# Layer norm 2 on ScalarE: variance as centred squares, two GpSimd operations a pair, and a newly written order

## The chip, the cores and the metric

The kernel runs on one core of a Trainium2 chip. Its engines work side by side: TensorE (PE; its weight loads are listed as PEld), VectorE (DVE), ScalarE (ACT), GpSimd (POOL) and SyncE (SP), which here issues every transfer. The metric is the device time of one execution in microseconds, the median of several runs.

## The reference, cut to what matters

One input `x` (2048 tokens, 640 channels, bf16) goes through two branches, and a gate mixes them.

```python
g = sigmoid((x * gate_w).sum(-1, keepdims=True))
# branch A: a gated long convolution over the tokens
kv = (four-tap shift convolution of k with shift_k) * v
y  = irfft(rfft(kv padded to 2S) * rfft(ssm_k padded to 2S))[:S] + kv * ssm_D
a  = x * y
# branch B: a token-shift MLP
h  = gelu(layernorm(x) @ w1)
x1 = x + concat(four channel groups of h, shifted by 1, -1, 2, -2 tokens) @ w2
b  = x1 + gelu(layernorm(x1) @ w3) @ w4          # w3: 640x1536, w4: 1536x640
out = g * a + (1 - g) * b
```

`layernorm` subtracts the mean over the channels and divides by the root of the variance plus 1e-5. The second one, of `x1`, is "layer norm 2" here.

## The kernel before

Tokens lie as 128 partitions by 16 slabs; a slab `s` is 128 tokens by 640 channels. The work is cut into small named nodes, and the names carry the slab or chunk.

Branch B. `st0.s` are the statistics of layer norm 1, `rs0.s` the root for a pair of slabs, `xn0.s` the normalised slab. It is transposed into XNT, on TensorE (`tr`, evacuated by `te`) or by a transposing transfer (`xt0.c.i`). `W1.c.n` multiplies chunk `c` (four slabs) by w1, `g1` is the GELU, `mx` the shift of the mixed rest, `gt` and `z` the gate. `W2.s` multiplies by w2, and `add s` (L674) adds to QX and sums the row into SSM. Then `st1.s`, `rs1.s`, `xn1.s`, `xt1.c.i` are layer norm 2 with its transposes; its chunks begin with slabs 2, 6, 10 and 14. `W3.c.f` and `g2.c.f` follow, `W4.s.j` with the addition `w4e.s.j` (L784). `xo s` scales x1 by 1 - g.

Branch A computes the long convolution as a two-step discrete Fourier transform in matrix form. `trh`, `trhe` transpose the filter; `h1.c.u` is its first step, `he` the evacuation, `hw c` the write to DRAM. `km`, `ka`, `kv` are the shift convolution of k times v on VectorE (L828 to L840); `x1.c.u`, `xe`, `xw c` its first step. `rh` and `rx` read both back in another layout, `h2`, `x2` are the second step, evacuated by `h2e`, `x2e`. `sw` swaps two halves of the filter's spectrum by transfer. `pq` (L912) multiplies the spectra, `pv` starts the inverse, `ve` evacuates, `vw` writes, `rv` reads, `iv` ends the inverse, `ye`, `y`, `ya` gate and add it, `st s` stores.

What sets the order: no scheduler runs when the kernel is built. A string, ORDER, lists all nodes; a word is a name, an engine letter (P, A, V, G, S) and the places in the buffers that it uses. Each engine takes its nodes in the order of that string, one after the other, so a node that waits holds up all that stand behind it on its engine. SyncE's nodes are the issues of transfers, and what it issues runs in one queue. PSUM has eight places; an evacuation frees one or two of them for the next matmuls. The numbers in braces in `pl.add` ("plan times", ns) are what a planner outside this file used when it wrote ORDER; in the kernel they do nothing.

Layer norm 2 before: `st1` is one ScalarE instruction, a square scaled by D to the power of -1/2 with the row sum into SSQ. `rs1` is five GpSimd operations on 128x2: mean from SSM, its square, the difference from SSQ, plus epsilon, power of -1/2. `xn1` (L534, VectorE) subtracts the mean and multiplies by the root.

Of the kernel before, what the change touches and what calls it, by code (L numbers as in the profile page):

```python
# [9 lines left out]
ACT = mybir.ActivationFunctionType  # L10
ALU = mybir.AluOpType
# [74 lines left out]
h0/S bpi/V idn/G warm/P/0 iw/G cw/V is/G dz/G cs/V ang1/V and1/V sin1.1/A abs1/A sin1.0/A ang0/V and0/V sin0.1/A abs0/A  # L86
sin0.0/A q1/S st0.3/V st0.2/V h2/S h4/S q0/S st0.0/A m3i0/G trh0/P/2 trhe0/V/2 misc/G st0.1/V rs0.2/G xn0.3/V/0 xn0.2/V/1
trh2/P/4 trhe2/A/4 trh4/P/6 rs0.0/G h1/S q3/S st0.6/V st0.7/A rs0.6/G trh1/P/0 tr0.0.2/P/2/0/1/0 trhe1/A/0 trhe4/V/6 xn0.1/V/2
xn0.0/V/0 h3/S trh3/P/4 te0.0.2/V/2/0 tr0.0.0/P/6/0/0/2 te0.0.0/A/6/0 trhe3/V/4 h1.2.2/P/2/0 he.2.2/A/2/0 iz/G m3i1/G w1/S
h1.3.0/P/0/1 h1.2.0/P/4/0 he.2.0/A/4/0 W1.0.1/P/6/0 q2/S st0.5/V he.3.0/A/0/1 st0.4/V xn0.6/V/1 xn0.7/V/0 q4/S st0.9/V st0.8/V  # L90
q7/S h1.1.0/P/2/2 h1.2.1/P/4/0 he.1.0/A/2/2 W1.0.0/P/7/0 he.2.1/A/4/0 tr0.1.2/P/0/1/1/0 te0.1.2/V/0/1 rs0.4/G xn0.4/V/2
xn0.5/V/0 q5/S tri/S w2b2/S q6/S W1.0.2/P/2/0 W1.0.3/P/3/0 tr0.1.0/P/4/1/2/0 te0.1.0/V/4/1 w1m/G gw/S gt.0/P/0/0 rs0.8/G
xn0.9/V/1 st0.14/V g1.0.1/A/6 st0.12/V xn0.8/V/0 st0.15/A st0.11/A st0.10/V W1.0.4/P/1/0 z0/V/0 w2a/S st0.13/V g1.0.2/A/2
rs0.14/G W1.1.0/P/6/1 g1.1.0/A/6 g1.0.4/A/1 W1.1.4/P/4/1 g1.1.4/A/4 mx1.1/V mx0.1/V g1.0.0/A/7 g1.0.3/A/3 W1.1.3/P/2/1
g1.1.3/A/2 mx0.2/G rs0.10/G cjb/S drow/S hw2/S/0 W1.1.1/P/6/1 g1.1.1/A/6 w2b3/S kb1/S/0 xt0.2.1/S/0/1 w2b1/S mx1.3/V m3i3/G
xn0.11/V/2 w2b0/S xt0.2.0/S/0/0 h1.0.1/P/4/0 he.0.1/A/4/0 h1.1.2/P/0/2 he.1.2/A/0/2 k1.0/S/1 xt0.2.3/S/0/2 h1.3.2/P/2/1
he.3.2/V/2/1 xn0.10/V/1 mx0.0/G xt0.2.2/S/0/1 W1.1.2/P/7/1 g1.1.2/A/7 gt.1/P/6/1 h1.1.1/P/2/2 h1.0.2/P/4/0 he.0.2/A/4/0 z1/V/6
he.1.1/A/2/2 hw1/S/2 h1.3.1/P/0/1 xn0.14/V/0 xt0.3.2/S/1/0 W2.4/P/6 add4/V/6 W2.2/P/4 add2/V/4 W2.3/P/2 ka1/S/0 he.3.1/A/0/1
hw3/S/1 xn0.15/V/2 xt0.3.3/S/1/2 kb0/S/0 cj2/A cj0/A ic0/A W1.2.3/P/0/0 m3b/V g1.2.3/A/0 W1.2.1/P/1/0 st1.4/A g1.2.1/A/1 m3i2/G
m3i4/G cj3/G kz/V/0 rs0.12/G mx1.2/G mx1.0/G add3/V/2 xn0.12/V/1 xt0.3.0/S/1/1 xn0.13/V/0 xt0.3.1/S/1/0 gt.2/P/0/0 ka2/S/0  # L100
z2/V/0 ka0/S/0 cj1/A h1.4.2/P/6/2 he.4.2/A/6/2 h1.4.1/P/4/2 he.4.1/A/4/2 h1.0.0/P/2/0 he.0.0/A/2/0 hw0/S/0 W2.5/P/0 add5/V/0
ic1/V st1.5/A v0.1/S m3c/G m3d/V W1.2.4/P/6/0 g1.2.4/A/6 mx2.3/V h1.6.0/P/4/1 h1.6.1/P/0/1 he.6.1/V/0/1 he.6.0/A/4/1
h1.6.2/P/2/1 he.6.2/A/2/1 hw6/S/1 v0.0/S W1.2.2/P/7/0 g1.2.2/A/7 st1.2/A W1.2.0/P/6/0 st1.3/A gt.3/P/2/1 W1.3.4/P/3/1
g1.3.4/A/3 W1.3.0/P/7/1 g1.3.0/A/7 g1.2.0/A/6 W1.3.2/P/3/1 g1.3.2/A/3 z3/V/2 gate0/V gate1/A rs1.4/G xn1.5/V/2 xt1.0.3/S/0/2
W1.3.3/P/2/1 g1.3.3/A/2 w3/S h1.5.2/P/4/0 he.5.2/A/4/0 h1.5.1/P/0/0 he.5.1/A/0/0 h1.5.0/P/6/0 he.5.0/A/6/0 km0.0.3/V/0/0
km0.0.2/V/0/0 km0.0.1/V/0/1 xn1.4/V/1 ka0.0.2/V/0/0 gate2/V km0.0.0/V/0/0 ka0.0.1/V/1/0 ka0.0.0/V/0/0 rs1.2/G mx2.2/G
W1.3.1/P/3/1 g1.3.1/A/3 mx2.0/G xn1.2/V/0 kv0/V/0 xt1.0.2/S/0/1 W2.6/P/4 add6/V/4 xn1.3/V/2 xt1.0.1/S/0/2 h1.7.0/P/0/1
h1.4.0/P/6/2 mx2.1/G he.4.0/A/6/2 W2.7/P/2 add7/V/2 st1.7/A xt1.0.0/S/0/0 W2.8/P/6 W2.9/P/4 km0.1.3/V/0/0 km0.1.2/V/0/1
add8/V/6 he.7.0/A/0/1 st1.6/A mx3.1/G mx3.3/G W2.12/P/2 m3s/A mx3.2/G add9/V/4 mx3.0/G W2.11/P/0 h1.7.2/P/6/1 he.7.2/A/6/1
st1.8/A st1.9/A xo4/A add12/V/2 km0.1.1/V/0/0 ka0.1.2/V/1/0 ka0.1.1/V/0/0 rs1.6/G xn1.7/V/1 add11/V/0 km0.1.0/V/0/1  # L110
ka0.1.0/V/1/0 st1.12/A kv2/V/0 xn1.6/V/2 k1.1/S/1 km1.0.3/V/1/0 km1.0.2/V/1/0 ka1.0.2/V/0/0 km1.0.1/V/1/1 ka1.0.1/V/1/0
km1.0.0/V/1/0 ka1.0.0/V/0/0 v1.1/S v1.0/S kv4/V/0 h1.7.1/P/4/1 he.7.1/A/4/1 rs1.8/G xn1.9/V/0 mx0.3/G km1.1.3/V/1/0
km1.1.2/V/1/1 km1.1.1/V/1/0 ka1.1.2/V/1/0 w4/S xt1.1.0/S/1/2 W2.13/P/2 W3.0.11/P/6/0/0 g2.0.11/A/6/0 W3.0.3/P/7/0/1
W3.0.9/P/0/0/0 g2.0.3/A/7/1 g2.0.9/A/0/0 W3.0.6/P/1/0/2 W3.0.2/P/4/0/1 g2.0.2/A/4/1 xo3/A W3.0.1/P/5/0/1 xo6/A W3.0.0/P/0/0/1
g2.0.1/A/5/1 add13/V/2 xo7/A W3.0.4/P/4/0/2 g2.0.4/A/4/2 W3.0.5/P/5/0/2 g2.0.5/A/5/2 W3.0.7/P/4/0/2 g2.0.6/A/1/2 ka1.1.1/V/0/0
km1.1.0/V/1/1 g2.0.0/A/0/1 g2.0.7/A/4/2 W3.0.10/P/5/0/0 ka1.1.0/V/1/0 st1.11/A g2.0.10/A/5/0 W3.0.8/P/0/0/0 g2.0.8/A/0/0
kv6/V/0 xn1.8/V/2 st1.13/A rs1.12/G W2.10/P/6 add10/V/6 st1.10/A rs1.10/G k2.1/S/0 k2.0/S/0 km2.0.3/V/0/0 km2.0.2/V/0/0
xt1.1.1/S/1/1 v2.0/S v2.1/S xo9/A xo2/A ka2.0.2/V/0/0 xt1.1.3/S/1/0 W4.2.0/P/0/1/2/0 W4.3.1/P/1/1/2/0 km2.0.1/V/0/1
km2.0.0/V/0/0 W4.3.0/P/2/1/2/0 w4e3.1/V/1 w4e3.0/V/2 W4.2.1/P/3/1/2/0 W4.4.0/P/4/1/2/0 xt1.1.2/S/1/2 w4e2.1/V/3 ka2.0.1/V/1/0
ka2.0.0/V/0/0 xn1.13/V/1 w4e2.0/V/0 kv8/V/0 v3.0/S hw5/S/0 k3.1/S/1 W4.4.1/P/1/1/2/0 W4.5.1/P/5/1/2/0 xo5/A w4e5.1/V/5  # L120
W3.1.3/P/0/1/3 g2.1.3/A/0/3 W4.5.0/P/5/1/2/0 km2.1.3/V/0/0 km2.1.2/V/0/1 w4e4.1/V/1 w4e5.0/V/5 ka2.1.2/V/1/0 W3.1.1/P/0/1/3
hw4/S/2 W3.1.10/P/1/1/0 g2.1.10/A/1/0 xn1.12/V/0 g2.1.1/A/0/3 xt1.2.3/S/0/1 w4e4.0/V/4 W3.1.4/P/5/1/1 g2.1.4/A/5/1 k3.0/S/1
hw7/S/1 x1.0.2/P/6/0 x1.0.1/P/2/0 xe.0.1/A/2/0 x1.0.0/P/0/0 xe.0.0/A/0/0 xe.0.2/A/6/0 xw0/S/0 v3.1/S xn1.10/V/2 km2.1.1/V/0/0
xt1.2.0/S/0/2 km2.1.0/V/0/1 ka2.1.1/V/0/0 ka2.1.0/V/1/0 kv10/V/0 W3.1.5/P/4/1/1 g2.1.5/A/4/1 W3.1.0/P/5/1/3 g2.1.0/A/5/3
x1.1.0/P/2/2 xe.1.0/A/2/2 x1.1.2/P/0/2 W3.1.7/P/6/1/1 g2.1.7/A/6/1 xe.1.2/A/0/2 W3.1.8/P/7/1/0 g2.1.8/A/7/0 x1.1.1/P/4/2
xe.1.1/A/4/2 xw1/S/2 xn1.11/V/1 km3.0.3/V/1/0 xt1.2.1/S/0/1 xt1.2.2/S/0/0 km3.0.2/V/1/0 km3.0.1/V/1/1 ka3.0.2/V/0/0
x1.3.1/P/2/1 x1.3.0/P/0/1 xe.3.0/A/0/1 xe.3.1/V/2/1 ka3.0.1/V/1/0 km3.0.0/V/1/0 ka3.0.0/V/0/0 kv12/V/0 W3.1.9/P/6/1/0
g2.1.9/A/6/0 W3.1.2/P/7/1/3 g2.1.2/A/7/3 km3.1.3/V/1/0 km3.1.2/V/1/1 ka3.1.2/V/1/0 x1.4.0/P/4/0 xe.4.0/A/4/0 km3.1.1/V/1/0
km3.1.0/V/1/1 ka3.1.1/V/0/0 ka3.1.0/V/1/0 kv14/V/0 x1.4.1/P/2/0 xe.4.1/A/2/0 x1.4.2/P/0/0 xe.4.2/A/0/0 xw4/S/0 W3.1.6/P/6/1/1
g2.1.6/A/6/1 W3.1.11/P/7/1/0 x1.3.2/P/4/1 xe.3.2/A/4/1 xw3/S/1 x1.6.0/P/2/2 W2.0/P/0 xe.6.0/A/2/2 x1.6.1/P/4/2 x1.6.2/P/2/2  # L130
xe.6.2/A/2/2 xe.6.1/A/4/2 xw6/S/2 g2.1.11/A/7/0 xo10/A W3.2.0/P/6/0/2 g2.2.0/A/6/2 W2.1/P/2 add1/V/2 st1.1/A W3.2.1/P/7/0/2
xo8/V g2.2.1/A/7/2 rh1/S/0 add0/V/0 st1.0/A W2.15/P/4 x1.5.0/P/2/0 xe.5.0/A/2/0 x1.2.0/P/0/1 xe.2.0/A/0/1 add15/V/4 st1.15/A
W2.14/P/6 add14/V/6 st1.14/A W3.2.2/P/2/0/2 g2.2.2/A/2/2 rh0/S/1 x1.5.1/P/4/0 xe.5.1/V/4/0 x1.5.2/P/0/0 xe.5.2/V/0/0 xw5/S/0
# [43 lines left out]
def kernel(  # L177
# [16 lines left out]
    nc = tc.nc  # L194
# [808 lines left out]
```

## Time and profile before

| | |
|---|---|
| median of 5 runs | 231.18 us (228.54 to 232.07) |
| the profiled execution | 231.4 us |
| its span, first to last instruction | 229.6 us |
| granted TensorE clock | 0.994 |
| busy: PE, DVE, ACT, POOL | 212.9, 177.5, 170.3, 53.7 us |
| bytes moved | 65.39 MB, 285 GB/s on average |
| `rs1` and `rs0`: power of -1/2 (L527) | 16 of 824 ns on average |
| `rs1`: mean (L523) | 8 of 497 ns |
| `st1`: square (L507), its read of the sum | 16 of 738 ns, 16 of 193 ns |
| `xo`: copy with a pointer scale (L688) | 12 of 829 ns |
| gate activation, 128x16 (L640) | 1 of 208 ns |
| PSUM evacuation 128x1024, ScalarE, VectorE | 1.03 us (KV), 1.06 us on average (SX) |

Busy times say how full an engine is, not who holds up whom. TensorE is busy 93% of the span; the profile models the ends of its matmuls. A wait is told as "who <- what ended it". Start times below are microseconds from the span's start.

### The profile page before, as it was taken

What the parts mean: (1) busy time and instruction counts of PE and PEld (TensorE: products, weight loads), DVE (VectorE), ACT (ScalarE), POOL (GpSimd) and SP (SyncE); (2) the same over time, 40 slices, a digit from 0 to 9 for tenths busy, and PEclk for the clock granted to TensorE, in tenths of its full rate; (3) what the DMA queues carried; (4) which work ended last, traced back from release to release, by engine and by line L of the source; (5) the groups of instructions that cost most, each with busy time, mean ns of one, the idle gap of its engine ahead of it and who ended that gap; (6) DMA issues with size and microseconds to landing.
All of it is one profiled execution on the core that took longest, in us unless ns stands there. A gap on an engine that the chain in (4) does not pass through costs nothing.

```text
span 229.6 us, 4842 instructions
## 1 busy us (share of the span) xinstructions
PE 212.9 (93%) x1849; PEld 120.0 (52%) x1849; DVE 177.5 (77%) x311; ACT 170.3 (74%) x251; POOL 53.7 (23%) x129
## 2 busy tenths in 40 slices
PE   7999996999899998999999997997989999999990
PEld 7974553554654475644555554332435554466660
DVE  6799875579999999999996792778945887018991
ACT  5899995898399925169889941898997998517750
POOL 5276391659754057000004000000000000000000
PEclk9999999999999999999999999999999999999997
DMA  7999999989989999987999999999998949689995
GB/s 236 379 385 167 342 209 201 292 245 317 280 189 293 276 213 183 288 222 197 270 295 375 381 241 383 202 355 361 273 377 259 387 168 316 233 307 402 344 359 192
DMA packets 51095, 65.39 MB, mean 285 GB/s; under 512 B 20608, under 2 KB 37761, under 8 KB 50688
## 3 DMA queue, kind: packets, MB, share of 16 engines
q1 hardware_dynamic: 51072, 65.09, 97.8%
q8 instruction: 14, 0.23, 0.4%
q14 instruction: 9, 0.07, 0.1%
HBM read 37.03 MB, written 18.35 MB: 241 GB/s over the span
## 4 chain that ended last, share of the span: by engine, by line
PE 58%; DVE 19%; DMA 12%; issue 4%; SPq 3%; ACT 1%; DVEq 0%; POOL 0%; POOLq 0%
PE PS L778 15%; PE PS L765 14%; DMA R<-R 7%; PE PS L667 6%; PE PS L861 6%; DMA XNT<-XN 5%; PE PS L578 4%; PE PS L701 4%; DVE RK L833 4%; PE PS L726 4%; DVE RK L837 4%; SPq L541 3%; PE PS L946 2%; PE PS L472 2%; DVE XN L534 1%
## 5 line engine op out<-in xcount | busy, mean ns | idle before, releaser
L330 ACT CAST SX<-PS 128x1024 bf16<-128x1024 f32 (+1 forms) x58 | 51.3, 933 | 9.4 <-PE PS L861 7.8
L778 PE MATMUL PS<-W,RG 128*128 128x320 bf16 x384 | 56.0, 299 | 1.4 <-DVE QX L784 1.0
L765 PE MATMUL PS<-XNT,W 128*128 128x512 bf16 x240 | 56.0, 380 | 0.3 <-DMA XNT<-XN 0.2
L778 PEld LDWEIGHTS <-RG 128*128 128x128 bf16 x384 | 36.4, 98 | 21.2 <-issue 7.0
L769 ACT ACTIVATE RG<-PS 128x512 bf16<-128x512 f32 x48 | 28.2, 609 | 13.7 <-PE PS L765 13.4
L765 PEld LDWEIGHTS <-W 128*128 128x128 bf16 x240 | 22.0, 98 | 29.6 <-issue 5.4
L784 DVE SCALAR_TENSOR_TENSOR QX<-PS,ZG,QX 128x320 bf16<-128x320 f32 x32 | 17.0, 547 | 20.2 <-PE PS L778 17.7
L912 DVE TENSOR_TENSOR SX<-SX,R 128x2048 bf16<-128x2048 bf16 x20 | 23.8, 1221 | 7.0 <-DMA R<-R 5.9
L578 PE MATMUL PS<-XNT,R 128*128 128x512 bf16 x100 | 23.2, 379 | 2.3 <-DMA XNT<-XN 2.3
L667 PE MATMUL PS<-R 128*128 128x320 bf16 x160 | 23.7, 299 | 0.9 <-DVE QX L674 0.8
L837 DVE TENSOR_TENSOR RK<-RK 128x1280 bf16<-128x1280 bf16 x24 | 20.4, 851 | 0.4
L667 PEld LDWEIGHTS <-R 128*128 128x128 bf16 x160 | 15.3, 98 | 9.3 <-issue 3.1
L833 DVE TENSOR_TENSOR RK<-RK,CJ 128x1280 bf16<-128x1280 bf16 x24 | 19.1, 818 | 0.0
L507 ACT ACTIVATE RG<-QX 128x640 bf16<-128x640 bf16 x16 | 11.8, 738 | 9.2 <-DVE QX L674 9.1
L330 ACT CAST KV<-PS 128x1024 bf16<-128x1024 f32 x17 | 17.2, 1029 | 1.7 <-PE PS L861 1.6
L534 DVE TENSOR_SCALAR XN<-QX,MV,RS 128x640 bf16<-128x640 bf16 x32 | 14.3, 461 | 3.0 <-DMA XNT<-XN 2.6
L674 DVE SCALAR_TENSOR_TENSOR QX<-PS,QX 128x640 bf16<-128x640 f32 x16 | 12.9, 814 | 4.7 <-PE PS L667 4.5
L861 PEld LDWEIGHTS <-M 64*64 64x64 bf16 x320 | 7.9, 105 | 15.8 <-issue 8.5
L861 PE MATMUL PS<-RK,M 64*64 64x512 bf16 x160 | 13.9, 386 | 2.5 <-DMA RK<-GXD 2.5
L578 PEld LDWEIGHTS <-R 128*128 128x128 bf16 x100 | 9.1, 97 | 13.4 <-issue 3.6
L585 ACT ACTIVATE R<-PS 128x512 bf16<-128x512 f32 x20 | 11.2, 611 | 3.9 <-PE PS L578 3.9
L523 POOL TENSOR_SCALAR MV<-ST 128x2 f32<-128x2 f32 x8 | 4.0, 497 | 43.2 <-DVE QX L674 43.0
(116 smaller groups left out, 281.8 us busy)
## 6 DMA issues: line engine op xcount, KB each, us to landing
GHD<-SX SPq DMA_DIRECT2D x8, 640.0 KB, 6.2
GXD<-SX SPq DMA_DIRECT2D x8, 640.0 KB, 4.5
RK<-GHD SPq DMA_DIRECT2D x4, 1280.0 KB, 8.8
RK<-GXD SPq DMA_DIRECT2D x4, 1280.0 KB, 8.0
R<-R SPq DMA_DIRECT2D x8, 640.0 KB, 7.8
VD<-KV SPq DMA_DIRECT2D x4, 1280.0 KB, 7.0
W<-in_B_w_dram SPq DMA_DIRECT2D x2, 1920.0 KB, 11.1
RK<-in_A_k_dram SPq DMA_DIRECT2D x6, 560.0 KB, 7.6
```

Of the source, the lines that this page charges most:

```text
L330: nc.scalar.copy(out=o, in_=i)
L534: xn = pl.add("xn%d.%d" % (i, s), {V: 360}, lambda e: nc.vector.tensor_scalar(out=XN[:, b.idx, :], in0=QX[:, s, :], scalar1=MV[:, i, s, 0: ...
L578: nc.tensor.matmul(ps(pb), lhsT=lhsT, rhs=XNT[:, xb.idx, k, :], start=(k == 0), stop=(k == DT - 1))
L667: nc.tensor.matmul(ps(pb)[:, j, 0:DH], lhsT=gst_ap(k, s), rhs=W2[:, k, j * DH:(j + 1) * DH], start=(k == 0), stop=(k == DT - 1))
L765: nc.tensor.matmul(ps(pb), lhsT=W3[:, k, f0 * P:(f0 + 1) * P], rhs=XNT[:, xb.idx, k, :], start=(k == 0), stop=(k == DT - 1))
L769: gns.append(pl.add("g2.%d.%d" % (c, f0), {A: act_p(512)}, lambda e, f0=f0, pb=pb, gb=gb: nc.scalar.activation(out=GTP[:, gb.idx, f0 % 4, ...
L778: nc.tensor.matmul(ps(pb)[:, 0:DH], lhsT=GTP[:, gbs[f // 4].idx, f % 4, i * P:(i + 1) * P], rhs=W4[:, f, j * DH:(j + 1) * DH], start=(f == ...
L784: nc.vector.scalar_tensor_tensor(out=x, in0=ps(pb)[:, 0:DH], scalar=OMG[:, s:s + 1], in1=x, op0=ALU.mult, op1=ALU.add)
L833: m = pl.add("km%d.%d.%d" % (c, u, j), {V: dve(2 * D, .52)}, lambda e, src=src, cj=cj, tb=tb: nc.vector.tensor_tensor(out=TMP[:, tb.idx].r ...
L837: prev = pl.add("ka%d.%d.%d" % (c, u, j), {V: dve(2 * D, .52)}, lambda e, tb=tb: nc.vector.tensor_tensor(out=acc, in0=acc, in1=TMP[:, tb.i ...
L861: nc.tensor.matmul(pt[64 * C:64 * C + 64, R, :], lhsT=M3[64 * R:64 * R + 64, m, :], rhs=rhs_fn(R, C), start=start, stop=stop)
L912: nc.vector.tensor_tensor(out=PQ[:, qb.idx], in0=XS[:, sb.idx].unsqueeze(1).to_broadcast([P, 2, 1024]), in1=HH[:, hhb.idx, u], op=ALU.mult)
```

## The change

Three things change.

First, the arithmetic of layer norm 2. `st1` on ScalarE becomes two instructions: the sum is scaled by -1/D, which gives minus the mean, and the square is taken of QX with that as its bias, so that the row sum is that of centred squares. `rs1` on GpSimd becomes two operations: scale by 1/D plus epsilon, and the power. `xn1` adds minus the mean where it subtracted the mean.

```diff
-                nc.scalar.activation(out=JNK if i else JN0, in_=QX[:, s, :], func=ACT.Square, scale=float(D) ** -0.5,
-                                     accum_out=SSQ[:, s:s + 1])
...
+                else:
+                    nc.scalar.activation(out=MV[:, i, s, 0:1], in_=SSM[:, s:s + 1], func=ACT.Copy, scale=-1.0 / D)
+                    nc.scalar.activation(out=JNK, in_=QX[:, s, :], func=ACT.Square, bias=MV[:, i, s, 0:1],
+                                         accum_out=SSQ[:, s:s + 1])
...
+                if i == 1:
+                    ve = VE[:, i, s0:s0 + 2]
+                    g.tensor_scalar(out=ve, in0=SSQ[:, s0:s0 + 2], scalar1=1.0 / D, scalar2=1e-5, op0=ALU.mult, op1=ALU.add)
+                    g.tensor_tensor(out=RS[:, i, s0:s0 + 2], in0=ve, in1=NHALF[:], op=ALU.pow)
+                    return
...
-                        if i == 1:
-                            g.tensor_scalar(out=m[:, :, 0], in0=SSM[:, a:b], scalar1=1.0 / D, scalar2=None, op0=ALU.mult)
...
-            op0=ALU.subtract, op1=ALU.mult), [rsn[(i, s0)]], [b])
+            op0=ALU.subtract if i == 0 else ALU.add, op1=ALU.mult), [rsn[(i, s0)]], [b])
```

Second, plan times: `m3c` 5000 to 6000, `iz` 3500 where it was 2200 (GpSimd), `rs1` 2300 to 1900, `st1` 735 to 930, `trh` 16 x 120 to 16 x 114.

Third, ORDER is written anew with these times: every engine has another order, with other buffer places. On the matrix side the same nodes stand in it. Some nodes change engine. To VectorE from ScalarE go he.0.0, he.0.2, he.1.1, he.1.2, he.2.2, he.3.1, he.4.1, he.4.2, trhe1, trhe2, st0.0, st0.11, st0.15, xo3, xo4, xo12, xo15, xe.5.0, xe.7.1, h2e.0.4, h2e.1.1, h2e.2.2, h2e.3.1, x2e.0.3, x2e.2.0, x2e.2.2. To ScalarE from VectorE go he.3.2, he.6.1, trhe4, te0.1.2, st0.1, st0.4, st0.13, st0.14, ic1, xo8, xe.3.1, xe.5.1, xe.5.2, h2e.0.2, h2e.0.3, h2e.1.2, h2e.2.4, h2e.3.2. The copies cj0 to cj2 go from ScalarE to GpSimd; mx0.0, mx0.3, mx1.0, mx1.2 and mx3.3 from GpSimd to VectorE, mx0.1 the other way.

Of SyncE's order, the two stretches that the prediction speaks of, before and after:

```diff
-hw1 xt0.3.2 ka1 hw3 xt0.3.3 kb0 xt0.3.0 xt0.3.1 ka2 ka0 hw0
+hw1 xt0.3.2 ka2 xt0.3.1 hw3 xt0.3.3 xt0.3.0 ka1 kb0 ka0 hw0
...
-xw5 xw2 xw7 rq0 xt1.3.2 xt1.3.3 rx0 sw0.1 sw0.0 rx1 xt1.3.0 xt1.3.1 sw1.1 sw1.0 rh2
+xw5 xw2 xw7 xt1.3.3 rq0 xt1.3.2 rx0 sw0.0 sw0.1 rx1 sw1.1 xt1.3.0 xt1.3.1 sw1.0 rh2
```

Of TensorE's order, three stretches:

```diff
-W2.6 h1.7.0 h1.4.0 W2.7 W2.8 W2.9 W2.12 W2.11 h1.7.2 h1.7.1 W2.13 W3.0.11
+W2.7 W2.6 W2.9 W2.8 h1.7.0 h1.4.0 W2.11 W2.12 W2.13 W3.0.11
...
-W2.10 W4.2.0 W4.3.1 W4.3.0 W4.2.1 W4.4.0 W4.4.1 W4.5.1 W3.1.3 W4.5.0
+W2.10 W4.4.0 W4.4.1 W4.5.1 W4.5.0 W4.3.1 h1.7.1 x1.1.2 h1.7.2 W4.2.0 W4.3.0 W4.2.1 W3.1.0
...
-W3.3.5 pv.3.2 pv.3.0 W3.3.4 W3.3.7 W3.3.6 W3.3.0 W3.3.1 W3.3.2 W3.3.3 W4.0.0
+W3.3.5 pv.3.2 pv.3.0 W3.3.6 W3.3.4 W3.3.2 W3.3.7 W3.3.3 W3.3.1 W3.3.0 W4.0.0
```

## The prediction

> **What bounds the kernel now.** I read the page's busy times first, then TensorE's waits, then busy time by stage, then the chain of waits.
>
> ```profile
> PE 212.9 (93%) x1849; PEld 120.0 (52%) x1849; DVE 177.5 (77%) x311; ACT 170.3 (74%) x251; POOL 53.7 (23%) x129
> q1 hardware_dynamic: 51072, 65.09, 97.8%
> ```
> Two resources are nearly full: TensorE, and the one transfer queue that SyncE feeds. Neither amount of work changes: the same 1849 matmuls with the same 88 changes between 64x64 and larger tiles, the same transfers. Only waits can move. TensorE's:
> ```profile
> PE PS L861 <- DMA RK<-GXD: 2.5, 2, 1.7
> PE PS L578 <- DMA XNT<-XN: 2.3, 1, 2.3
> PE PS L472 <- POOL IDN L467: 1.5, 1, 1.5
> PE PS L861 <- DVE SX L912: 1.3, 1, 1.3
> PE PS L778 <- DVE QX L784: 1.0, 1, 1.0
> PE PS L667 <- DVE QX L674: 0.8, 1, 0.8
> ```
> (us in all, times, longest.) With the smaller ones they make 10.6 us, and 6.0 us follow the last matmul. That is all there is to win. None waits for GpSimd's LN2 statistics. Who is full where:
> ```profile
> 50.00:61.00 11.00, 10.23 (x78) 5.26 (x76) 10.90 (x19) 7.10 (x13) 9.62 (x12) 1.00 1.06 352
> 61.00:118.00 57.00, 55.89 (x388) 30.21 (x387) 56.35 (x89) 40.99 (x69) 14.36 (x22) 1.00 0.98 236
> 140.00:158.00 18.00, 14.85 (x129) 5.97 (x129) 11.88 (x13) 13.60 (x17) 0.00 (x0) 1.00 1.11 314
> ```
> (Window, length, then busy PE, PEld, DVE, ACT, POOL, clock, DMA share, GB/s.) From 50 to 118 us VectorE never rests: its k-convolution sets when x1 and the reads `rh` start. From 140 to 158 us transfers set the pace; the chain there is:
> ```profile
> 143.51 3.79 SPq L541
> 147.35 0.60 SPq L895
> 148.00 7.45 DMA R<-R
> 155.57 1.24 DVE SX L912
> ```
> The issue of a transpose (`xt1.3.1`) keeps SyncE 3.8 us, the swap `sw1` queues behind it, and `pq.1.3` waits for the swap.
>
> **GpSimd statistics.** In a quiet stretch `rs1.4` took 2.46 us: 0.76, 0.20, 0.19, 0.26, 0.72. Two operations remain, about 1.55. Beside VectorE's convolution `rs1.12` took 3.97; two fifths to a half of it remain, about 2. The removal is worth 8 x 0.9 to 1.9 = 7 to 15 us of GpSimd, but VectorE waited for the power operation 0.3 us in all, so on the path 0 to 0.3; I take 0. What hides it is VectorE's backlog: `xn1.10`, ready at 91.1, ran at 99.4.
>
> **ScalarE statistics.** Each `st1` gains a 128x1 scale. Nearest row: the 128x16 gate activation, 208 ns. The square gets a pointer bias: nearest row the pointer-scaled `xo`, 829 ns against 738 without. [...] But the square reads what the scale writes, and where the trace has such a pair (`abs` after `sin`) it starts 30 ns after the end. By the rows: 0.21 + 0.03 + 0.09 = 0.33 each, 5.3 us. I take the rows. Queued behind are GELUs and evacuations, behind them PSUM slots. From 61 to 118 us ScalarE has 16 us free; the tightest place is `st1.0`, `st1.1`, then `g2.2.0`, whose slot `W3.2.2` wants at 121.05, and I get 120.5. Cost 0; without that cover 0.7.
>
> [...]
>
> **Evacuations change engines.** At the page's means VectorE gains 8.1 us and ScalarE loses 10.4 (with the scale, 5). Some 4 us of it lie before 49 us, where VectorE had about 13 us idle.
>
> **The new order, stage by stage.**
>
> *0 to 39.5.* I laid the new order on the row durations. Behind h4, one load later, `trh4` waits 0.2; W1.0.3 starts at 17.75, W2.3 at 32.9 (before: W1.0.1 17.41, W2.4 32.99). Ahead of `xt0.2.2` stand exactly the same transfers; its input is ready at 32.8 (before 32.86), so it lands at 39.3 again and W1.2 starts at 39.5. Effect 0, bounds -0.5 to +0.3 (us won).
>
> *39.5 to 48.* `kb0` and `ka1` move behind the four `xt0.3`: their last landing falls from 48.05 to about 46. gt.3 starts at 47.5, not 48.5, but 0.75 us of h1.6 are left for later: +0.25.
>
> *48 to 118.* VectorE reaches the end of add6 at 61.0 (before 60.78), with xn1.3, xo4 and mx3.3 also done. Back-to-back operations overlap: from add6 to kv14 the row means of before add to 61.35 us and took 56.96, a factor of 0.93. The new list adds to 60.2, so 55.9: kv14 at 116.9 against 117.74. TensorE's waits for it: h1.7.0 0.55, h1.4.0 0.4 (both for PSUM slots that W2's adds clear), W3.0.2 0.35 (add11 sits behind ten convolution steps), W4.5.0 0.65: 1.95 against 0.77 + 0.09 + 1.03. h1.7.1 and h1.7.2 move behind W4.3.1; their write hw7 then goes at 92 instead of 95.85, and v3.0, v3.1 behind it still land before kv12 needs them. `iz` and the `ic` copies fall into free time. Net about +0.4 with the 0.25: TensorE would be ready for x2 at 139.65, before at 140.07.
>
> *118 to 142.* Before, x2 waited 1.69 us for rx0 (landed 141.72), which waits for the last x write. Here kv14 is 0.8 us earlier, xw5 can go at 122.4 (was 124.98) and xw7 at 126.6 (128.56); the queue runs at its 338 to 370 GB/s throughout. rx0 then lands at about 140.7: +1.05, between 0 (queue unchanged) and 2.1 (TensorE alone decides).
>
> *142 to 165.* `sw1.1` goes ahead of `xt1.3.0` and `xt1.3.1`; these get their input only at 142.9 (xn1.14 follows x2e.0.3; before 137.5). I put the landing of sw1.0 at 152.5 to 154 (before 155.45). pv.1.3, 13.25 us of matmul after x2, could start at 153.95; with the product's 1.3 us I take 154.5 against 156.85: +2.35 so far, bounds +0.5 to +3. The loop h2.2, rx2, x2.2 keeps its 0.7 us wait.
>
> *165 to 203.* x2e.2.0 and x2e.2.2 now run on VectorE between the products, 1.2 us each: pv.2.3 comes 0.5 and pv.2.2 0.2 late: -0.7 (0 to -1.2). g2.3.0, whose tile the first matmul of W4.0.0 reads, becomes the last GELU; before it was g2.3.3, and three matmuls ran ahead (W4.0.0 took 2.09 pitch instead of 1.63). Now 0.16 + 0.67 = 0.83 is lost instead of 0.45: -0.4.
>
> *The tail.* Reads `rv` at 1.65 us each stay ahead of `iv`; after W4.0.1 the same add and store follow: 0.
>
> Sum: +2.35 - 0.7 - 0.4 = about 1.3 us. The profiled execution took 231.4 (span 229.6), so 230.1 here; the median of the five runs stands 0.2 below it: **229.8 us**. About 1% (2.3 us) is what a measurement here can tell from no change.
>
> **Rivals.**
> 1. *The read chain gains in full* (chance 0.2): x2 starts at 139.65, pv.1.3 does not wait, the losses after 165 vanish behind the next transfer. 2.1 + 1.26 + 0.4 = 3.8 us: 227.4. For it: the 2 us stretch from 147 to 149 in which the queue moved only 25 GB/s, which the earlier sw1.1 may fill.
> 2. *It does nothing on the time* (0.19): rx0 does not land earlier, because the queue before it was full anyway, and pv.1.3 merely inherits its wait: 231.2. For it: 97.8% of the queue.
> 3. *VectorE becomes the longer bound* (0.23): if the 4 us added ahead of z3 don't fit its gaps, or new evacuations stand before an add that holds PSUM, all from add6 on shifts one for one through kv14 to rh1. It decides from add6 ending after about 62.5; at 64 the sum is 3 us later, less part of the gain: 233.7. Against: those 13 us idle before 49.
>
> Forecast 0.38. Its own range is 228.3 to 231.4. Eight in ten reaches to most of rivals 1 and 3: **226.9 to 233.9**. Faster by over 1% (under 228.9): rival 1 and a third of the forecast, 0.33. Slower by over 1% (over 233.5): most of rival 3 and a tail, 0.21. Within 1%: 0.46.
>
> **What the new profile would show.** Right: W1.2 still starts near 39.5 behind a transpose; add6 ends by 61.5 and kv14 by 117.5, VectorE idle below 1 us between them; wait on GXD at most 1.1 us; the swap's wait before pq.1.x shorter than 2.2 us; W4.0.0 waits 0.5 us or more for L774's GELU. Wrong: kv14 after 119, x2 after 141.7, or a new wait for the transposes of the last chunk (W3.3.11), since xn1.14 and xn1.15 now come 5 us later.

## The result and the profile after

The changed kernel took 228.96 us (median of 39 runs, 225.85 to 233.14), the kernel before beside it 231.07 us (74 runs). The ratio, which here and below compares only those executions of a kernel that lie within 1.5% of its fastest, is 0.990, with a 95% interval of 0.988 to 0.992: about 2.3 us faster, where the medians over all executions differ by 2.1. I had said 229.8 (the sum in my working gives 229.9).

The profiled execution took 231.2 us (span 229.4). For 3.4 us of it TensorE's granted clock was 0.50, so it serves here for the order of events, and a second profile (E1, span 224.7) for the durations.

Busy times and the queue, first of the changed kernel:

```profile
PE 214.2 (93%) x1849; PEld 120.9 (53%) x1849; DVE 185.9 (81%) x321; ACT 167.2 (73%) x259; POOL 39.5 (17%) x107
q1 hardware_dynamic: 51072, 65.09, 97.5%
```

GpSimd lost 14 us and VectorE gained 8; the work of TensorE and of the queue is what it was. TensorE's waits (us in all, times, longest):

```profile
PE PS L770 <- DMA XNT<-XN: 2.2, 1, 2.2
PE PS L471 <- POOL IDN L466: 1.5, 1, 1.5
PE PS L866 <- DMA RK<-GXD: 1.4, 1, 1.4
PE PS L783 <- ACT RG L774: 0.7, 1, 0.7
...
PE PS L583 <- DVE XN L539: 0.4, 1, 0.4
PE PS L866 <- DVE SX L917: 0.3, 1, 0.3
```

Against before, the 2.3 us ahead of W1.2 are 0.4 us. The row at L583 names VectorE, but W1.2 waits for the transpose xt0.2.2, as before: it starts 0.13 to 0.14 us after that transfer lands in every profile of the new order (here it lands at 38.66 and W1.2 starts at 38.80), also in E13 below, where VectorE's xn had ended 0.7 us earlier. The wait for the swapped spectrum (L917, was 1.3) is 0.3, and a new one of 2.2 us stands at L770: W3.3.11 waits for the transposes of the last chunk. The 1.4 us behind GXD are no longer rx0 but rx2, late behind the stretch of half clock; E1 has no wait there. The stages (window, length, busy PE, PEld, DVE, ACT, POOL, clock, DMA share, GB/s):

```profile
50.00:61.00 11.00, 10.64 (x76) 6.09 (x74) 10.76 (x20) 8.94 (x14) 4.57 (x7) 1.00 1.07 331
61.00:118.00 57.00, 55.45 (x391) 30.06 (x391) 56.31 (x90) 44.94 (x77) 7.50 (x11) 1.00 1.00 246
140.00:158.00 18.00, 15.83 (x127) 5.96 (x125) 13.56 (x15) 11.86 (x15) 0.00 (x0) 0.91 1.11 293
```

VectorE is as full as before from 50 to 118 us, and kv14 ends at 117.4 us (117.7). ScalarE does 4 us more there and still has 12 us free. The chain from 140 us on (start, us, what):

```profile
133.02 6.82 DMA RK<-GXD
...
141.55 0.79 DVE XN L539 x2
142.34 0.51 DVE QX L789
142.85 0.90 SPq L546
143.76 0.04 issue
143.80 8.52 DMA XNT<-XN
152.32 0.05 issue
152.36 1.86 PE PS L770 x5
```

Before, this chain ran through the swap. Now it runs through xn1.14 and xn1.15 and the transpose xt1.3.1, issued at 143.8 and landed at 152.3. Behind the wait the granted clock falls:

```profile
150.20:152.30 2.10, 0.00 (x0) 0.00 (x0) 1.54 (x2) 1.76 (x2) 0.00 (x0) 1.00 0.80 207
152.90:156.20 3.30, 3.30 (x15) 0.78 (x14) 2.06 (x2) 0.93 (x2) 0.00 (x0) 0.50 1.07 368
156.40:158.00 1.60, 1.60 (x20) 0.54 (x19) 0.17 (x1) 1.05 (x2) 0.00 (x0) 1.00 0.84 290
```

2.1 us with no matmul, then 3.4 us at 0.50, which cost an estimated 3.4/2 = 1.7 us: in them eight 64x64 matmuls of the inverse (L866, from 154.15 us) took 1.07 us, and the next eight at full clock (157.12) 0.60.

### The profile page after: what moved, and what is told of

Read it like the earlier page. It is cut to its first block, busy times and chain, and to the rows that moved or that the text cites. A ratio compares the mean times of both kernels' runs of the same rounds, so it can differ in the third digit from the quotient of the medians.

```text
span 229.4 us, 4819 instructions
## 1 busy us (share of the span) xinstructions
PE 214.2 (93%) x1849; PEld 120.9 (53%) x1849; DVE 185.9 (81%) x321; ACT 167.2 (73%) x259; POOL 39.5 (17%) x107
## 4 chain that ended last, share of the span: by engine, by line
PE 34%; DMA 29%; DVE 16%; ACT 6%; SPq 5%; issue 5%; POOL 3%; DVEq 0%; POOLq 0%; ACTq 0%
PE PS L770 12%; PE PS L783 11%; DMA XNT<-XN 6%; DMA RK<-in_A_k_dram 5%; PE PS L866 5%; DMA QX<-in_A_q_dram 4%; DMA R<-R 4%; DMA RK<-in_A_shift_k_dram 3%; DMA RK<-GXD 3%; DMA GXD<-SX 3%; PE PS L672 3%; DVE RK L842 3%; DVE RK L838 2%; DVE QX L971 2%; DMA GHD<-SX 2%
## 5 line engine op out<-in xcount | busy, mean ns | idle before, releaser
L770 PE MATMUL PS<-XNT,W 128*128 128x512 bf16 x240 | 56.9, 385 | 2.7 <-DMA XNT<-XN 2.2
L783 PE MATMUL PS<-W,RG 128*128 128x320 bf16 x384 | 55.9, 299 | 0.8 <-ACT RG L774 0.7
L329 ACT CAST SX<-PS 128x1024 bf16<-128x1024 f32 (+1 forms) x50 | 43.8, 928 | 12.5 <-PE PS L866 9.9
L770 PEld LDWEIGHTS <-W 128*128 128x128 bf16 x240 | 22.1, 99 | 33.6 <-issue 8.1
L774 ACT ACTIVATE RG<-PS 128x512 bf16<-128x512 f32 x48 | 27.6, 608 | 10.5 <-PE PS L770 10.3
L917 DVE TENSOR_TENSOR SX<-SX,R 128x2048 bf16<-128x2048 bf16 x20 | 24.1, 1221 | 5.2 <-DMA R<-R 4.6
L583 PE MATMUL PS<-XNT,R 128*128 128x512 bf16 x100 | 23.4, 379 | 0.9 <-ACT XNT L329 0.5
L672 PE MATMUL PS<-R 128*128 128x320 bf16 x160 | 23.1, 299 | 0.9 <-DVE ZG L606 0.5
L333 DVE CAST SX<-PS 128x1024 bf16<-128x1024 f32 (+1 forms) x18 | 19.2, 1069 | 4.6 <-PE PS L866 3.1
L838 DVE TENSOR_TENSOR RK<-RK,CJ 128x1280 bf16<-128x1280 bf16 x24 | 20.1, 852 | 0.0
L672 PEld LDWEIGHTS <-R 128*128 128x128 bf16 x160 | 15.5, 98 | 8.1 <-issue 1.8
L539 DVE TENSOR_SCALAR XN<-QX,MV,RS 128x640 bf16<-128x640 bf16 x32 | 14.1, 455 | 3.3 <-POOL RS L532 2.6
L866 PEld LDWEIGHTS <-M 64*64 64x64 bf16 x320 | 8.1, 106 | 14.3 <-issue 8.6
L583 PEld LDWEIGHTS <-R 128*128 128x128 bf16 x100 | 9.1, 97 | 11.7 <-issue 1.4
L518 POOL TENSOR_SCALAR VE<-ST 128x2 f32<-128x2 f32 x8 | 1.8, 229 | 76.9 <-ACT RG L509 76.8
L866 PE MATMUL PS<-RK,M 64*64 64x512 bf16 x160 | 13.5, 386 | 1.5 <-DMA RK<-GXD 1.4
L331 ACT ACTIVATE R<-PS 128x1024 bf16<-128x1024 f32 x14 | 13.9, 1037 | 1.0 <-PE PS L866 0.9
L731 PE MATMUL PS<-KV,F 64*64 64x128 bf16 (+1 forms) x256 | 13.2, 304 | 1.3 <-DVE QX L679 0.7
```

Of the source, the lines that this page charges most:

```text
L329: nc.scalar.copy(out=o, in_=i)
L333: nc.vector.tensor_copy(out=o, in_=i)
L583: nc.tensor.matmul(ps(pb), lhsT=lhsT, rhs=XNT[:, xb.idx, k, :], start=(k == 0), stop=(k == DT - 1))
L672: nc.tensor.matmul(ps(pb)[:, j, 0:DH], lhsT=gst_ap(k, s), rhs=W2[:, k, j * DH:(j + 1) * DH], start=(k == 0), stop=(k == DT - 1))
L770: nc.tensor.matmul(ps(pb), lhsT=W3[:, k, f0 * P:(f0 + 1) * P], rhs=XNT[:, xb.idx, k, :], start=(k == 0), stop=(k == DT - 1))
L774: gns.append(pl.add("g2.%d.%d" % (c, f0), {A: act_p(512)}, lambda e, f0=f0, pb=pb, gb=gb: nc.scalar.activation(out=GTP[:, gb.idx, f0 % 4, ...
```

## The experiments

All do the whole computation. Ratios are to the kernel before, run beside them.

### E1: the changed kernel again

No edit.

> The changed kernel once more, for a profile whose granted clock is undisturbed between 140 and 165 us. Theory (the read chain gives the gain, the clock only disturbed the first profile): the wait of W3.3.11 for the transposes of the last chunk is there again, 1.5 to 2.5 us, sw1.0 lands at 153.5 to 154.5, and pv.1.3 starts at 155.3 to 155.8 (157.12 in the first profile, 156.85 before); span 226 to 228. Rival (the half clock is part of this order, brought on by that wait): the granted clock falls again in the 4 us behind the wait, and pv.1.3 stays at 157.

Measured: 227.6 us, ratio 0.9896 (0.985 to 0.995); span 224.7. Its wait at W3.3.11 and its stage:

```profile
PE PS L770 <- DMA XNT<-XN: 1.7, 1, 1.7
```
```profile
140.00:158.00 18.00, 16.28 (x144) 6.34 (x142) 15.55 (x17) 14.47 (x20) 0.00 (x0) 1.00 1.13 316
```

The wait of W3.3.11 is part of the kernel, the half clock is not part of every execution: the mean granted clock of these six was 0.995 or more. Span, sw1.0's landing (152.4) and the start of pv.1.3 (153.9) fell below what I expected; this execution was 0.5 us ahead of the first one at 18 us and 1 us at W1.2. From the start of x2 to pv.1.3 it took 15.18 us, where before took 15.09. The exchange in the queue brought the swap no sooner: sw1.0 landed 13.7 us after x2 started, as before, and the wait only stands at another matmul.

### E2 and E3: arithmetic alone, order alone

E2 has the new functions with the old string ORDER:

```diff
-ORDER = """
-idn/G warm/P/0 bpi/V h0/S trh0/P/2 iw/G is/G dz/G m3i2/G
...
+ORDER = """
+h0/S bpi/V idn/G warm/P/0 iw/G cw/V is/G dz/G cs/V
...
```

> The new arithmetic (scale and biased square on ScalarE, two GpSimd operations a pair) in the order of the kernel before. My theory: hidden on both engines, the ratio to before is 0.999 to 1.003; GpSimd busy falls from 53.7 by 7 to 15 us, ScalarE's rises by 5.3. Rival 1 (fewer GpSimd operations beside VectorE are what shortens the kernel): the whole gain, about 0.990. Rival 2 (the scales delay GELUs and evacuations): +0.7 us or more, 1.003 or above.

Measured: ratio 1.0041 (1.001 to 1.007). GpSimd fell from 53.7 to 41.2 us, as expected, and ScalarE rose by 4.0, less than the 5.3, but the time is 0.9 us longer: my theory missed, and the time is that of rival 2. TensorE has new waits for ScalarE; before had none of these three:

```profile
PE PS L771 <- ACT SX L330: 0.9, 2, 0.6
...
PE PS L771 <- ACT RG L775: 0.6, 1, 0.6
...
PE PS L732 <- ACT SX L330: 0.4, 1, 0.4
```

W3.0, W3.2 and x1.7 wait 1.9 us for PSUM slots that ScalarE clears late, 0.56 us of it at W3.2.2, the place that I had called the tightest. That they are the 0.9 us is not shown: x2, which comes behind them all, starts only 0.3 us later than before, and another 0.8 us is lost between pv.1.3 and W4.0.0, where this profile waits 0.9 us for rh3.

E3 is the reverse, the new ORDER with the old functions:

```diff
-ORDER = """
-h0/S bpi/V idn/G warm/P/0 iw/G cw/V is/G dz/G cs/V
...
+ORDER = """
+idn/G warm/P/0 bpi/V h0/S trh0/P/2 iw/G is/G dz/G m3i2/G
...
```

> The new order with the arithmetic of before (one square on ScalarE, five GpSimd operations a pair). My theory: the order carries the gain, ratio 0.989 to 0.992; rs1.14 takes 1.5 us longer, but xn1.15 stands behind x2e.0.3 anyway. Rival (the arithmetic carries it): 1.000; a mixed case, in which the longer rs1.14 makes xn1.15 and so the transposes later, 0.994 to 0.996.

Measured: ratio 0.9928 (0.990 to 0.996). The order carries most of the gain, 1.7 of 2.3 us. From kv14 on E3's profile is that of E1 within 0.3 us up to the tail; it is 2 us later at W1.2. So I ran it again:

> The new order with the arithmetic of before, a second time, because its first profile reached W1.2 1 to 2 us later than every profile of the changed kernel (first W1.2 at 39.96 us against 37.84 to 39.01), although no statistics of layer norm 2 run before 40 us. If that was chance in the queue (my theory): first W1.2 at 37.8 to 39.1, ratio 0.989 to 0.992. If the arithmetic reaches that stage in some way: W1.2 again at 39.5 or later, ratio 0.992 to 0.995.

Measured: ratio 0.9924 (0.989 to 0.996), W1.2 at 39.70 us. My theory of chance missed again. This profile has a stretch of half clock from 15 to 18.5 us, but E11's has one too and reaches W1.2 at 38.70. (The premise was wrong in one point: st1.3 does run before 40 us, at 37 to 39 us, but behind W2.3 and add3, which are late already.) So the arithmetic is worth +0.9 us in the old order and perhaps -0.6 us in the new one, where the intervals overlap. Through what it reaches W1.2 I could not find: until 36 us all engines execute the same instructions in E1, E3 and E13, and xt0.2.2, issued at 33.2, 34.8 and 34.4 us, lands at 37.7, 39.8 and 39.6.

### E4: the scale on VectorE

```diff
                                            accum_out=SSM[:, s:s + 1])
+            nc.vector.tensor_scalar(out=MV[:, 1, s, 0:1], in0=SSM[:, s:s + 1], scalar1=-1.0 / D, scalar2=None, op0=ALU.mult)
...
-                    nc.scalar.activation(out=MV[:, i, s, 0:1], in_=SSM[:, s:s + 1], func=ACT.Copy, scale=-1.0 / D)
```

> The changed kernel with the mean's scale on VectorE behind each add (16 operations of 128x1) and the biased square alone on ScalarE. My theory (VectorE's convolution is the bound from 50 to 118 us): some 12 scales of 0.1 to 0.15 us before kv14 put it 1.2 to 1.8 us later (about 119 us), x2 starts as much later, and the time is 0.8 to 1.8 us above the changed kernel: ratio to before 0.993 to 0.998. [...]

Measured: ratio 1.004 (1.001 to 1.007), 3.2 us above the changed kernel. The costs of the scale on either engine, E4's VectorE and the changed kernel's ScalarE (mean ns of one):

```profile
L680 DVE TENSOR_SCALAR MV<-ST 128x1 f32<-128x1 f32 x16 | 2.5, 154 | 0.6
```
```profile
L509 ACT ACTIVATE RG<-QX,MV 128x640 bf16<-128x640 bf16 x16 | 13.2, 828 | 0.6
L508 ACT ACTIVATE MV<-ST 128x1 f32<-128x1 f32 x16 | 3.2, 197 | 6.5 <-DVE QX L679 6.5
L509 ACT ACTIVATION_READ_ACCUMULATOR RG<-QX,MV 128x1 f32 x16 | 3.0, 186 | 0.0
```

VectorE's is the shorter instruction and the dearer place: kv14 ended at 119.85 us against 116.4 to 117.6 in the profiles of the changed kernel. Direction as expected, size double: 12 scales ahead of kv14 make 12 x 0.154 = 1.85 us, and the start up to W1.2 was about 1 us later, as in E3, for a reason that is as open here.

### E5: the new wait undone

```diff
-... rx1/S/1 x2.0.3/P/6/0/0 x2e.0.3/V/6/0 xn1.15/V/0 xn1.14/V/2 ... sw1.1/S/0 xt1.3.0/S/1/2 xt1.3.1/S/1/0
+... rs1.14/G xn1.15/V/0 xn1.14/V/2 ... rx1/S/1 xt1.3.0/S/1/2 xt1.3.1/S/1/0 x2.0.3/P/6/0/0 ... sw1.1/S/0
```

> The changed kernel with xn1.15 and xn1.14 right behind rs1.14 and their transposes ahead of sw1.1 in SyncE's order. Theory (from x2 on the one queue is the limit, and W3.3.11's new wait only stands in the place of the swap's wait): W3.3.11 waits below 0.5 us, but pq.1.3 still starts some 13.8 us after x2 because sw1.0 lands no sooner, pv.1.3 stays 14.8 to 15.3 us after x2's start (15.18 in the changed kernel), and the time is that of the changed kernel, ratio to before 0.988 to 0.992. Rival (the late transposes themselves cost the gain of the swap): pv.1.3 comes 13.3 to 13.7 us after x2 and the ratio is 0.983 to 0.985.

Measured: 228.7 us, ratio 0.9899 (0.984 to 0.996), no change against the changed kernel that six executions could show. The waits changed places:

```profile
PE PS L865 <- DVE SX L916: 1.9, 2, 1.6
...
PE PS L769 <- DMA XNT<-XN: 0.7, 1, 0.7
```

W3.3.11 waits 0.7 instead of 1.7, pv.1.3 waits 1.6 for its product, and pv.1.3 starts 15.9 us after x2 (expected 14.8 to 15.3). Both waits stand for the same transfers: between 140 and 154 us the queue moves rx1, two swaps and two transposes. But the queue is not full all that time. Before, in the changed kernel and in E9 (the order of before in this stage; last number GB/s):

```profile
147.00:149.00 2.00, 2.00 (x25) 0.68 (x21) 2.00 (x3) 2.00 (x3) 0.00 (x0) 1.00 0.07 25
```
```profile
148.00:151.00 3.00, 2.19 (x25) 0.88 (x21) 3.00 (x5) 3.00 (x5) 0.00 (x0) 1.00 0.93 38
```
```profile
146.00:149.00 3.00, 3.00 (x32) 1.11 (x25) 3.00 (x4) 3.00 (x5) 0.00 (x0) 1.00 1.16 305
```

The earlier sw1.1 did not fill the pause, as rival 1 had hoped. The pause goes with the swap's landing: sw1.0 landed 13.7 and 14.1 us after x2 started with 2 and 3 us of it, 12.9 us in E9 without it. No run removes it on purpose, and what causes it stays open. This run also undoes the swap's place ahead of the transposes, to which I had given 1.3 us.

### E6, E8, E12: less in the queue

One load of q, rq0 (0.33 MB), is moved from ahead of rx0: in E6 and E8 behind sw1.0, in E12 behind vw2. E6 and E12 start from the changed kernel, E8 from the kernel before.

```diff
-... xt1.3.3/S/1/2 rq0/S/0 xn1.0/V/1 ... sw1.0/S/0 ...
+... xt1.3.3/S/1/2 xn1.0/V/1 ... sw1.0/S/0 rq0/S/0 ...
```

> The changed kernel with one load, rq0 (0.33 MB, needed only at 203 us), moved from ahead of rx0 to behind sw1.0 in SyncE's order. Theory (what stands in the queue ahead of rx0 and the swaps sets the stage from 140 to 155 us): rx0 and sw1.0 land 0.7 to 0.9 us sooner against the start of x1.7 and pv.1.3 follows; ratio to before 0.986 to 0.988. Rival (the queue has room there, issue and TensorE set the pace): nothing, 0.990. Third case (the load only collides with vw0, rh2 or rx2 instead): the gain at pv.1.3 is there but lost again by x2.2, 0.990.

> The kernel before with rq0 alone moved behind sw1.0 in SyncE's order, nothing else. Theory (TensorE's wait for rx0, 1.69 us, is a queue wait): rx0 lands 0.7 to 0.9 us sooner, x2 starts as much sooner, ratio 0.996 to 0.998. Rival (the wait passes on to the swap, whose landing the queue sets anyway, or rh2 comes later): 1.000.

> The changed kernel with rq0 behind vw2 in SyncE's order (issued near 183 us) instead of ahead of rx0. Theory (behind sw1.0 it gained 1.1 us up to pv.1.3 and gave most back by delaying rh2; here the queue has a pause before vw3): x2 to pv.1.3 14.0 to 14.3 us, pv.1.3 to W4.0.0 44.0, ratio 0.985 to 0.987. Rival (the loop of swap and rx2 takes the gain back by itself, whatever stands in the queue): pv.1.3 to W4.0.0 44.6 to 45.0, ratio 0.989 to 0.991.

Measured: E6 0.987 (0.981 to 0.993), E8 1.003 (0.998 to 1.007), E12 0.990 (0.987 to 0.994). E6's profile shows 14.1 us from x2 to pv.1.3, 1.1 less than E1, and 44.8 instead of 44.0 from there to W4.0.0, so most is given back; but E11, with rq0 in its old place, took 14.3 up to pv.1.3, so one profile does not show that the move did it. In E12 the second number is 44.0, but the first 14.9. E8 missed: its rx0 landed 6.9 us after xw7, before 8.15, and the time is not shorter. E2 and E9, with rq0 in its old place, show 6.6 and 6.3, so the move gained nothing here that can be seen. None differs in time from its own parent beyond the intervals. In all seven profiles with the new order and the new arithmetic x2 starts 22.3 to 22.5 us after kv14, with rq0 ahead of rx0 or not. In five of them rx0 lands 0.1 to 0.8 us before x2 and TensorE sets it; in the changed kernel's first profile and in E11 rx0 lands 0.04 us before x2, so the queue is never far behind.

### E9 and E10: the tails exchanged

E9 is the kernel before up to W4.0.0 with the new order from there on; E10 the changed kernel with the old order from there on. The part that differs most:

```diff
-... rv5/S/6 ... rq4/S/2 ... rq5/S/3 ... rv6/S/0 ... st5/S ... st7/S rq6/S/1 ... st14/S st6/S st9/S st3/S ...
+... rv5/S/5 ... rq7/S/0 ... rv4/S/6 ... rq5/S/3 ... rv6/S/0 st2/S rq4/S/2 st6/S rq6/S/1 st15/S st1/S ...
```

> The order of the kernel before up to W4.0.0, and from there on (inverse, last W4 blocks, products, reads and stores) the new order; the old arithmetic. Theory (the tail, which I had put at 0, carries a good part of the gain): W4.0.0 to the end of W4.0.1 takes 21.9 us instead of 22.8, what follows it 4.9 to 5.1 instead of 5.4 to 6.1, and the ratio is 0.992 to 0.995. Rival (my step on the tail, 0): 22.8 and 5.4 to 6.1 again, or the same end by another wait; 0.999 to 1.001.

> The changed kernel up to W4.0.0, and from there on the order of the kernel before (its first two loads of q in this part, rq1 and rq3, included). Theory (half of the gain lies in the tail, as the old kernel with the new tail says at 0.9949): the end comes 0.8 to 1.3 us later, ratio 0.993 to 0.996. Rival (the tail's gain needs nothing of it, or the reads come early enough here for any tail): 0.990.

Measured: E9 0.9949 (0.991 to 0.999), E10 0.9951 (0.992 to 0.999). The tail is worth 1.2 us given to the old kernel, and as much taken from the new one, each give or take 0.9. SyncE's issues over time, before and then E1 (start, us, line, form, count):

```profile
214.21 0.52 SPq L934 DMA_DIRECT2D RK<-VD  x1
215.85 0.82 SPq L968 DMA_DIRECT2D out_dram<-QX  x2
216.72 0.49 SPq L938 DMA_DIRECT2D CJ<-in_A_q_dram  x1
217.31 8.73 SPq L968 DMA_DIRECT2D out_dram<-QX  x14
```
```profile
209.33 0.52 SPq L939 DMA_DIRECT2D RK<-VD  x1
209.90 0.59 SPq L973 DMA_DIRECT2D out_dram<-QX  x1
...
214.66 7.70 SPq L973 DMA_DIRECT2D out_dram<-QX  x14
```

In the old order the last read rv6 lands at 220.62 us and iv12 starts at 220.66; the last 14 stores take 8.7 us to issue, and st0 goes 0.93 us after its data are ready. In E1 rv6 lands 2.2 us before iv12, the 14 issues take 7.7 us, and st0 goes at once. TensorE needs 17.01 us from iv0 to the end of W4.0.1 in every profile with the new tail, 17.4 to 17.8 with the old one, and 4.9 to 5.5 us follow against 4.8 to 6.1. How much of it the reads do and how much the stores was not tested apart; TensorE shows no wait above 0.2 us for a read there.

### E11: two evacuations back on ScalarE

```diff
-x2e.2.0/V/6/1 ... x2e.2.2/V/4/1
+x2e.2.0/A/6/1 ... x2e.2.2/A/4/1
```

> The changed kernel with the evacuations x2e.2.0 and x2e.2.2 back on ScalarE. My step (on VectorE they make pv.2.3 and pv.2.2 late, 0.7 us): 0.3% faster than the changed kernel, 0.986 to 0.987. Rival (both engines have room there, TensorE has W4 blocks to run in the meantime): no difference, 0.989 to 0.991, and from pv.2.1 to W4.0.0 TensorE takes 25.0 us as in the changed kernel.

Measured: ratio 1.011 (1.004 to 1.018), 4.8 us above the changed kernel. Neither theory.

```profile
PE PS L865 <- DVE SX L916: 3.6, 2, 3.3
```
```profile
180.00:181.00 1.00, 0.00 (x0) 0.00 (x0) 0.00 (x0) 1.00 (x2) 0.00 (x0) 1.00 1.05 367
...
183.00:184.00 1.00, 1.00 (x12) 0.24 (x4) 1.00 (x2) 0.23 (x1) 0.00 (x0) 0.50 0.77 305
```

In ScalarE's list x2e.2.2 now stands behind x2e.3.1, which waits for matmuls of the next chunk; it ran 6.8 us after pv.2.1 began, in E1 3.1, pq.2.2 as much later, and pv.2.2 waited 3.3 us. Then the clock was halved for 3.4 us. 3.3 + 1.7 = 5.0 us fits the loss, and the half clock is no accident of this profile: five of the six executions had a mean granted clock of 0.980 to 0.988 and took 232.3 to 235.3 us, the sixth had 0.998 and took 230.7. The run shows what a place in a list costs, and says nothing of the two engines. That my step was wrong is seen in E1 itself: no wait ahead of pv.2.3 or pv.2.2.

## Why the prediction was right in its number and wrong in its parts

Stages from the profiles, in us. "Old" is the order of before (before, E2, E8, E9), "new" the new order with the new arithmetic (the changed kernel, E1, E5, E6, E10, E11, E12); where a kernel was edited within a stage, or a wait or half clock of its own disturbed it there (the changed kernel's first profile behind x2, E11 behind pv.1.3), it is left out. "Predicted" is what the working gives for the same stage.

| stage | old | new | gain | predicted |
|---|---|---|---|---|
| start to first W1.2 | 39.5 to 39.8 | 37.8 to 39.0 | 1.1 | 0 |
| first W1.2 to the end of kv14 | 78.1 to 78.9 | 78.5 to 78.6 | -0.1 | 0.84 |
| kv14 to x2 | 22.6 to 24.0 | 22.3 to 22.5 | 1.0 | 0.2 |
| x2 to pv.1.3 | 14.3 to 15.6 | 14.3 to 15.2 | 0.2 | 1.3 |
| pv.1.3 to iv0 | 49.2 to 50.0 | 48.9 to 49.4 | 0.3 | -1.1 |
| iv0 to the end of W4.0.1 | 17.4 to 17.5 | 17.0 | 0.4 | 0 |
| W4.0.1 to the end | 4.8 to 6.1 | 4.9 to 5.2 | 0.5 | 0 |

*GpSimd statistics, cost 0.* The amount was right: 12.5 to 14 us of work gone, inside my 7 to 15. In the old order it bought nothing (E2). In the new one the arithmetic may bring some 0.6 us (E3 and E13 against the changed kernel; the intervals overlap), by a way that stays open.

*ScalarE statistics, cost 0.* The unit was right: 0.197 + 0.03 + 0.09 against 0.33 us each, and the square did not overlap with the scale that it reads from: one st1, from its start to the end of the read, took 1.14 to 1.20 us, with 0.03 us idle in it (0.09 in one). In the new order none of E2's three waits for ScalarE appears, so the cover was there. In the old one it was not: 1.9 us of new waits and 0.9 us lost in all, where I had written 0.7, though the waits are not shown to be all of the loss.

*The scale on VectorE.* Right in direction: E4 costs 3.2 us, where I had expected 0.8 to 1.8; about 1 us of it stands ahead of W1.2 and is not explained.

*0 to 39.5.* Failed. The same transfers stand ahead of xt0.2.2, but it landed at 37.7 to 38.9 us, not at 39.3, in every profile of the new order with the new arithmetic, and W1.2 started right behind it. In the first profile it was not even issued earlier: at 34.07 us, before at 32.89, so it took 4.6 us instead of 6.4. Why is open. Here the same list of transfers did not land at the same time.

*39.5 to 118.* Right on the clock, by luck: add6 ended at 61.2 us (61.0), kv14 at 117.4 (116.9), since W1.2 came 0.7 us early. Counted from W1.2, kv14 took 78.6 us, before 78.2, where I had 77.4. The list from add6 to kv14 did get shorter, 56.2 for 56.97 us (I had 55.9), but add6 came 22.4 us after W1.2, before 21.3, where I had 21.5. So about 0.9 us of rival 3 was there, behind a start that hid it. TensorE waited 1.5 us for the adds' lines (0.7 at L731, 0.5 at L770, 0.3 at L672), where I had 1.95.

*118 to 142.* Right in kind: xw7 went at 126.9 us (126.6), and x2's wait for rx0 fell from 1.69 to 0.15 us. The size is not: of my 1.05 us, 0.84 were to come with kv14 and 0.2 in this stage, which gained 1.0. And the wait before was a long one: E2, E8 and E9, with the same order here, waited 0, 0.8 and 0.3 us. My "338 to 370 GB/s throughout" was a misreading too: from 133 to 136 us the queue moved 171 GB/s.

*142 to 165.* Failed, and this is the wrong step: I let sw1.1 pass the transposes and counted 1.3 us, and only named the late xn1.14 and xn1.15 as what could go wrong. W3.3.11 waits 0.6 to 2.5 us for them in the kernels that keep this place; the sign of being wrong that I had named came. The exchange gained nothing since sw1.0 landed no sooner: 13.7 us after x2 before and in E1 (12.9 to 14.2 in the old order, 12.7 to 14.5 in the new one), where I had about 12.6. E5 undid it at no cost that shows: reordering only moved the wait from pv.1.3 to W3.3.11.

*165 to 203.* Failed. x2e on VectorE lost 0, not 0.7 (the 1.2 us for one was right: VectorE's 128x1024 evacuations take 1.22 us; the 1.06 in the table of before mixes in smaller ones). W4.0.0 waits the 0.7 us that I foresaw, but before it lost as much: a 0.28 us wait and a pitch of 2.1 instead of 1.6 us within it.

*The tail, 0.* Failed: 1.2 us by E9 and by E10. I compared the matmuls and the last store, not when the reads land and how many stores are queued ahead of the last one.

So the number was right by luck. Against the sum in my working, the start gave 1.1 us more, VectorE's stage 0.9 less, the reads of x 0.8 more, the swap 1.1 less, the losses up to the tail 1.4 less, and the tail 0.9 more.

The stage gains sum to 3.4 us, the kernels differ by 2.3. The "old" column holds E2 and E8, which took 0.9 and 0.6 us more than the kernel before. The half clock is not the reason: among executions with a mean granted clock of 0.993 or more the medians are 228.3 us for the changed kernel and 230.3 for the kernel before (as run beside E1 to E4), 2.0 apart. The rest stays open.

## What to carry to other kernels

When two waits hang on one queue, ask whether the last transfer lands sooner, not which of them goes first; here it landed about 13.5 us into the stage in either order, and the wait only changed its place. Before believing a stage's time, count it from the stage's own start, in more than one profile. When an order is rewritten, test arithmetic and order apart: here the same arithmetic cost 0.9 us in one order and nothing that can be seen in the other. A tail is more than its last matmul: see when the last read lands, and how long the stores ahead of the last one take to issue.

## What was not expected of the hardware

In three profiles a wait of TensorE cost 1.5 to 1.8 times its own length. Waits of 2.2 us (changed kernel), 2.5 us (E13) and 3.3 us (E11) were each followed by 3.4 us at a granted clock of 0.50, an estimated 1.7 us lost. E13, the wait and the stretch behind it:

```profile
151.90:154.30 2.40, 0.00 (x0) 0.00 (x0) 1.51 (x2) 1.73 (x2) 0.00 (x0) 1.00 1.27 132
...
155.40:156.40 1.00, 1.00 (x6) 0.18 (x8) 0.25 (x1) 0.00 (x0) 0.00 (x0) 0.50 1.07 372
```

In the same place waits of 1.7 us and less (E1, E5, E6, E10, E12) were not, nor were the 2.3 us ahead of W1.2 in the kernel before. In E6, E11 and E13 (mean granted clock 0.985, 0.985 and 0.984) such a stretch also lies between 11 and 19 us, after waits of 1.1, 0.9 and 0.9 us, and E12 (0.995) has the same wait of 1.1 us without it, so the length of one wait does not decide. It shows without a profile too: of the changed kernel's 39 executions 15 had a mean granted clock below 0.993 and a median of 231.2 us, the other 24 one of 228.3. What decides whether such a stretch follows, no run here tests.
